# Weights by whole rows with the step in the lower word, sketches side by side, and the first batch's features beside its keys

## The chip, the cores and the metric

The kernel runs on one core of a Trainium2 chip. The metric is the device time of one execution in microseconds. Before the change the median is 358.86 us over three runs (357.6 to 360.12). An execution counts as slow here when it took over 1.5% longer than the fastest of the same kernel. In the profile before the change TensorE does the matrix products (busy 274.9 of 357.9 us), ScalarE and VectorE the element-wise work (153.8 and 250.4 us).

## The reference, cut to what matters

```python
# q, k, v: (batch 4, heads 4, seq 1088, head_dim 32) float32;  S1, S2: (8, 32) float64
def phi(x):                                   # degree-2 sketch: 64 features
    a = einsum('rd,bhsd->bhsr', S1, x)
    b = einsum('rd,bhsd->bhsr', S2, x)
    return einsum('bhsi,bhsj->bhsij', a, b).reshape(..., 64)
q_p, k_p = phi(q), phi(k)
num = q_p @ (k_p^T v);   den = q_p . sum(k_p) + 1e-6
x = num / den                                 # (4, 1088, 128)
theta = x @ w_theta                           # then the mixing over tokens:
y = w_tok_r @ (x * cos(theta)) + w_tok_i @ (x * sin(theta))     # two 1088 x 1088 matrices, float64
u = x + y
out = u + maximum(u @ w_ch, 0)
```

The denominator can be small, so the kernel computes it in exact slices of 16-bit numbers (names with `sl`, `cz`, `mv`, `lv`, `fl`, `dn`). Other names in the profiles: `cm` is the matrix made from the products of a batch's keys, `mv` the matrix for the denominators that is made from it, `kp` and `qp` the features of keys and queries, `zst` the phases, which are `x` times the cosine or the sine of theta. The two mixing matrices come as 8-byte floats, 17 rows of 128 x 1088. Each is turned into 4-byte floats on the chip, which is the first thing that the change touches.

## The kernel before

`load_f32` loads half a row of 544 columns. ScalarE reads the higher word of each float and writes its scaled value into `wT`, then writes two 16-bit halves of a correction, `step`, into a tile of its own, where the two halves of a column lie side by side. VectorE shifts `wT` by 3 bits and adds the step.

```python
def load_f32(dst, src):
    ...
    st = stg.tile([P, PIECE], I64, tag="st", name="st")[:p, :n]      # PIECE = 544, pool of 4
    nc.sync.dma_start(st, src)
    lo, hi = split(st)                                               # the two 4-byte words, 8 bytes apart
    step = stg.tile([P, PIECE, 2], I16, tag="step", name="step", bufs=2)[:p, :n]
    x = dst.bitcast(I32)
    A.activation(dst, hi.bitcast(F32), AF.Copy, scale=2.0**-112)
    A.activation(step[:, :, 1].bitcast(F16), hi.bitcast(F32), AF.Copy, scale=2.0**-60)
    A.activation(step[:, :, 0], lo.bitcast(U32), AF.Copy, scale=2.0**-29)
    ts(x, x, 3, ALU.logical_shift_left)
    tt(V, x, x, step.rearrange("p n t -> p (n t)").bitcast(I32), ALU.add)
...
    with level("first"):
        load(0, "kqv")
        ...                                     # S1, S2 in two tiles, each with its own small operations
        query_slices(0)
        matrices(0)                             # ends with mv
        keys_values(0, spare)
        attention(0)                            # features, denominators, then numerator and x by group
```

A tile framework schedules all this: the program gives levels of priority, and the framework fixes one order of instructions per engine. Each engine then works through its queue in that order: in the profile after the change, VectorE stands still for 2.90 us at one operation although the next one in its queue is ready.

## Time and profile before

| | before |
|---|---|
| time, median | 358.86 us |
| span of the profiled run | 357.9 us |
| ScalarE busy from 0 to 115.9 us | 86.80 us (75%) |
| VectorE busy in the same stretch | 92.05 us (79%) |
| first product of the mixing | 115.87 us |
| from there to the end | 242.0 us |

ScalarE's timeline in the steady stretch, one half row (columns: start, length, engine, line, output and input):

```profile
60.87 0.69 ACT L134 ACTIVATE wT<-st 128x544 f32<-128x544 f32 x1
61.47 0.80 ACT L135 ACTIVATE step<-st 128x544 f16<-128x544 f32 x1
62.13 0.79 ACT L136 ACTIVATE step<-st 128x544 int16<-128x544 uint32 x1
62.79 0.67 ACT L134 ACTIVATE wT<-st 128x544 f32<-128x544 f32 x1
```

A half row occupies ScalarE for 1.92 us here, from 60.87 to 62.79 (1.89 us for the next ones).

### The profile page before, as it was taken

How to read it: one execution, taken by the hardware profiler on the slowest of the kernel's cores; microseconds unless marked ns; L12 is line 12 of the kernel's file. 1: busy time of each engine (PE TensorE's matmuls, PEld its weight loads, DVE VectorE, ACT ScalarE, POOL GpSimd, SP SyncE). 2: the span in 40 equal slices, each digit the busy share in tenths (PEclk: the TensorE clock that was granted, in tenths of full speed). 3: DMA queues.
4: the chain of work that ended last, by engine and by line, in shares of the span. 5: the costliest groups of instructions: out<-in, count | busy, mean ns of one | idle time of the engine just before them, and what ended most of it. 6: DMA issues, size and time to landing. Idle time of an engine off the chain costs nothing.

```text
span 357.9 us, 4021 instructions
## 1 busy us (share of the span) xinstructions
PE 274.9 (77%) x1355; PEld 192.1 (54%) x1355; DVE 250.4 (70%) x713; ACT 153.8 (43%) x313; POOL 0.7 (0%) x6
## 2 busy tenths in 40 slices
PE   0406680145327999999689999996999999999994
PEld 0304480023226676776357777674777766776562
DVE  4898886985996699559948794896589569542111
ACT  0799729997958442061134413312335131332000
POOL 0000000000000000000000000000000000000000
PEclk9999955556555899999969999997899999999998
DMA  7668447883720012020010122000000000000010
GB/s 289 214 229 269 153 145 243 293 304 108 238 59 4 2 65 69 0 67 3 22 40 2 65 66 70 21 22 20 0 0 3 0 9 15 22 20 0 0 44 18
DMA packets 11604, 28.78 MB, mean 80 GB/s; under 512 B 1216, under 2 KB 5568, under 8 KB 11584
## 3 DMA queue, kind: packets, MB, share of 16 engines
q1 hardware_dynamic: 11376, 28.51, 24.3%
q8 instruction: 10, 0.16, 0.2%
q14 instruction: 10, 0.08, 0.1%
q10 hardware_dynamic: 208, 0.02, 0.0%
HBM read 26.30 MB, written 2.23 MB: 80 GB/s over the span
## 4 chain that ended last, share of the span: by engine, by line
PE 69%; DVE 17%; ACT 8%; DMA 3%; issue 1%; ACTq 0%
PE y L566 36%; PE w L519 4%; PE acc L398 3%; ACT step L135 3%; PE w L539 2%; PE y L576 2%; PE y L398 2%; PE w L446 2%; ACT step L136 2%; DVE wT L93 2%; PE w L513 2%; PE w L388 2%; DMA s_t_st<-s_t 2%; PE acc L306 2%; PE w L447 2%; PE w L534 1%
## 5 line engine op out<-in xcount | busy, mean ns | idle before, releaser
L566 PE MATMUL y<-wT,zst 128*128 128x384 f32 (+1 forms) x384 | 134.8, 481 | 1.4 <-DVE zst L93 1.4
L566 PEld LDWEIGHTS y<-wT,zst 128*128 128x128 f32 x384 | 68.1, 193 | 30.6 <-DVE zst L93 2.3
L585 ACT COPY ot<-y 128x384 f32<-128x384 f32 (+2 forms) x16 | 6.0, 398 | 62.1 <-PE y L580 62.1
L135 ACT ACTIVATE step<-st 128x544 f16<-128x544 f32 (+1 forms) x35 | 27.8, 795 | 4.3 <-DVE wT L93 4.2
L93 DVE CUSTOM_DVE_ANT_0 wT<-wT,step 128x1088 uint16<-128x1088 uint16 x34 | 24.4, 718 | 5.8 <-ACT step L136 5.8
L519 PEld LDWEIGHTS w<-kvbd,qpT 128*128 128x128 f32 x144 | 21.6, 213 | 11.3 <-ACT qpT L517 10.4
L136 ACT ACTIVATE step<-st 128x544 int16<-128x544 uint32 (+1 forms) x35 | 27.4, 784 | 0.0
L519 PE MATMUL w<-kvbd,qpT 128*128 128x64 f32 x144 | 23.4, 297 | 3.2 <-ACT qpT L517 3.1
L134 ACT ACTIVATE wT<-st 128x544 f32<-128x544 f32 x34 | 22.9, 685 | 2.3 <-DMA st<-w_tok 2.2
L517 ACT COPY qpT<-w 128x256 f32<-128x256 f32 x36 | 12.9, 367 | 24.6 <-PE w L513 24.5
L513 PE MATMUL w<-ident,qp 128*128 128x128 f32 x72 | 14.6, 304 | 7.7 <-DVE qp L93 7.6
L93 DVE TENSOR_TENSOR uT<-xT,y 128x384 f32<-128x384 f32 (+1 forms) x12 | 6.3, 529 | 19.2 <-PE y L566 19.1
L97 DVE TENSOR_SCALAR tn<-w 128x384 f32<-128x384 f32 x12 | 6.7, 557 | 17.8 <-PE w L539 17.8
L536 ACT COPY xT<-w 128x384 f32<-128x384 f32 x12 | 5.7, 475 | 29.8 <-PE w L534 29.8
L449 ACT COPY lv<-w 128x384 f32<-128x384 f32 x36 | 14.9, 504 | 8.3 <-PE w L448 8.2
L513 PEld LDWEIGHTS w<-ident,qp 128*128 128x128 f32 x72 | 10.1, 170 | 9.8 <-ACT wT L134 8.1
L97 DVE TENSOR_SCALAR wT<-wT 128x544 int32<-128x544 int32 x34 | 14.6, 435 | 0.0
L446 PE MATMUL w<-mv,q 128*128 128x384 f16 x36 | 13.4, 372 | 0.8 <-DVE mv L93 0.8
L398 PEld LDWEIGHTS acc<-ld_v,kp 128*128 128x128 f32 x108 | 13.0, 192 | 1.5
L539 PEld LDWEIGHTS w<-w,xT 128*128 128x128 f32 x72 | 10.6, 215 | 5.2 <-ACT xT L536 4.5
L404 ACT COPY kvbd<-acc 64x64 f32<-64x64 f32 x6 | 1.2, 206 | 27.6 <-PE acc L398 27.6
L100 DVE SCALAR_TENSOR_TENSOR fl<-lv 128x864 f32<-128x864 f32 x4 | 4.2, 1054 | 12.3 <-ACT lv L449 12.3
(230 smaller groups left out, 523.5 us busy)
## 6 DMA issues: line engine op xcount, KB each, us to landing
st<-w_tok SPq DMA_DIRECT2D x34, 544.0 KB, 4.6
ld_k<-k_l SPq DMA_DIRECT2D x4, 576.0 KB, 4.0
ld_q<-q_l SPq DMA_DIRECT2D x4, 576.0 KB, 4.4
ld_v<-v_l SPq DMA_DIRECT2D x4, 576.0 KB, 3.8
out<-ot SPq DMA_DIRECT2D x8, 192.0 KB, 2.1
out<-ot SPq DMA_DIRECT2D x4, 128.0 KB, 1.8
st<-w_sq SPq DMA_DIRECT2D x1, 256.0 KB, 4.6
out<-ot SPq DMA_DIRECT2D x4, 32.0 KB, 1.8
```

Of the source, the lines that this page charges most:

```text
L93: eng.tensor_tensor(out=o, in0=a, in1=b, op=op)
L97: V.tensor_scalar(out=o, in0=a, scalar1=s1, scalar2=s2, op0=op0, **kw)
L134: A.activation(dst, hi.bitcast(F32), AF.Copy, scale=2.0**-112)
L135: A.activation(step[:, :, 1].bitcast(F16), hi.bitcast(F32), AF.Copy, scale=2.0**-60)
L136: A.activation(step[:, :, 0], lo.bitcast(U32), AF.Copy, scale=2.0**-29)
L398: nc.tensor.matmul(kv[:, n], kp[:, i * H + 2 * n:i * H + 2 * n + 2].rearrange("p h i j -> p (h i j)"), vn[:, c, 2 * n:2 * n + 2].rearrange ...
L446: nc.tensor.matmul(lp, q0, flat[:, 0:4 * W], start=True, stop=False, skip_group_check=True)
L449: A.copy(lv[:, :, :, c].rearrange("p l t n -> p (l t) n"), lp.rearrange("p (x n) -> p x n", n=HR))
L513: nc.tensor.transpose(tr[:, n * P:(n + 1) * P], qp[:, i * H + 2 * n:i * H + 2 * n + 2].rearrange("p h i j -> p (h i j)"), ident)
L519: nc.tensor.matmul(num[:, i * P + n * 2 * D:i * P + (n + 1) * 2 * D], qpT[:, n], kvbd[b][:, n], start=True, stop=True)
L539: nc.tensor.matmul(th[:, i * P:(i + 1) * P], xT[:, i * P:(i + 1) * P], w2[:, 0], start=True, stop=True)
L566: nc.tensor.matmul(yp[:, :t1 - t0], z, wT[:, i, t0:t1], start=(i == 0), stop=(i == NK - 1))
```

## The change

It has three parts. The weights are converted by whole rows, and the step is written back into the lower word of the staged float, which saves the step tile. S1 and S2 lie side by side in one tile and share their small operations, and their loads come before those of q and v. For the first batch, everything that does not need its matrix (the level sums of two of the three outputs, half of the denominator's slices and all three groups of numerators) is placed ahead of that matrix. The diff holds some edits beside these: later batches make their matrix before they slice their queries, the slices of keys and queries share one buffer, and the phases use whole staged rows as buffers. The core of the diff, cut at the "..." lines:

```diff
-        st = stg.tile([P, PIECE], I64, tag="st", name="st")[:p, :n]        # pool of 4 half rows
+        st = stg.tile([P, S], I64, tag="st", name="st")[:p, :n]            # pool of 3 rows
-        step = stg.tile([P, PIECE, 2], I16, tag="step", name="step", bufs=2)[:p, :n]
+        step = st.bitcast(I16).rearrange("p (n t) -> p n t", t=4)
         A.activation(dst, hi.bitcast(F32), AF.Copy, scale=2.0**-112)
+        A.activation(step[:, :, 0], lo.bitcast(U32), AF.Copy, scale=2.0**-29)
         A.activation(step[:, :, 1].bitcast(F16), hi.bitcast(F32), AF.Copy, scale=2.0**-60)
-        A.activation(step[:, :, 0], lo.bitcast(U32), AF.Copy, scale=2.0**-29)
-        tt(V, x, x, step.rearrange("p n t -> p (n t)").bitcast(I32), ALU.add)
+        tt(V, x, x, lo, ALU.add)
 ...
-            for n in range(0, S, PIECE):
-                load_f32(wT[:, i, n:n + PIECE], w_tok[i][:, n:n + PIECE])
+            load_f32(wT[:, i], w_tok[i])
 ...
-        query_slices(0)
         matrices(0)
-        keys_values(0, spare)
-        attention(0)
+        query_slices(0)
+        features_s(0)                      # levels of the two outputs that need no matrix
+        denominator_slices(0, 1, 2)
+        keys_values(0, spare)
+        nums = [numerator(0, g, spare) for g in range(NG)]
+        features_n(0)
+        denominator_slices(0, 2, 3)
+        denominators(0)
+        for g in range(NG):
+            mixed(0, g, nums[g])
```

## The prediction

> **What bounds the kernel now.** I read the page first (busy shares, the 40 slices, the groups), then the stretches (windows), then the timeline of each engine over the first 130 us.
>
> ```profile
> PE   0406680145327999999689999996999999999994
> DVE  4898886985996699559948794896589569542111
> ACT  0799729997958442061134413312335131332000
> ```
>
> Each digit is the busy tenth of 9 us. There are two stages. Up to about 117 us TensorE is a third to half busy while ScalarE and VectorE turn the 8-byte weights into floats and prepare the first batch. After that TensorE is full (227 us busy of the 241 us from 117 us to the end). The stage before sets when the full stretch begins; its end is the first product with the batch's phases, here `zst`:
>
> ```profile
> 66.67 0.17 DVE L192 TENSOR_REDUCE mn<-acc 128x1 f32<-128x8 f32 x1
> 77.27 0.29 DVE L93 TENSOR_TENSOR mv<-nz,hmf 128x128 f16<-128x128 f16 x1
> 85.95 1.06 DVE L100 SCALAR_TENSOR_TENSOR fl<-lv 128x864 f32<-128x864 f32 x1 [3.08 <-ACT lv L449]
> 105.29 0.56 DVE L93 TENSOR_TENSOR x<-w,rd 128x384 f32<-128x384 f32 x1
> 115.25 0.56 DVE L93 TENSOR_TENSOR zst<-x,tn 128x384 f32<-128x384 f32 x1 [2.46 <-ACT tn L546]
> 115.87 2.92 PE L566 MATMUL y<-wT,zst 128*128 128x384 f32 x4 [1.23 <-DVE zst L93]
> ```
>
> Columns are start, length, engine, instruction, and the idle time before it. The batch's matrix `mv` is ready at 77.6, the features at 86.3 (ScalarE's last copy), the normalized `x` at 105.3, the mixing starts at 115.9. Between 85.9 and 105.3 VectorE has no idle time: its own queue is the path. Weights run through the same queues:
>
> ```profile
> L135 ACT ACTIVATE step<-st 128x544 f16<-128x544 f32 x34 | 27.3, 804 | 4.3 <-DVE wT L93 4.2
> L136 ACT ACTIVATE step<-st 128x544 int16<-128x544 uint32 x34 | 27.0, 793 | 0.0
> L93 DVE CUSTOM_DVE_ANT_0 wT<-wT,step 128x1088 uint16<-128x1088 uint16 x34 | 24.4, 718 | 5.8 <-ACT step L136 5.8
> L134 ACT ACTIVATE wT<-st 128x544 f32<-128x544 f32 x34 | 22.9, 685 | 2.3 <-DMA st<-w_tok 2.2
> L97 DVE TENSOR_SCALAR wT<-wT 128x544 int32<-128x544 int32 x34 | 14.6, 435 | 0.0
> ```
>
> That is 77 us of ScalarE and 39 us of VectorE in a stage of 117. The DMA waits (2.2 us) say that transfers do not bound it. TensorE is cold there:
>
> ```profile
> 48.56 5.79 PE L398 MATMUL y<-ld_v,kp 128*128 128x64 f32 x26
> 98.09 1.97 PE L519 MATMUL w<-kvbd,qpT 128*128 128x64 f32 x8
> 123.73 0.66 PE L519 MATMUL w<-kvbd,qpT 128*128 128x64 f32 x4
> ```
>
> Eight passes take 1.97 us at a granted clock of 0.50 (window 98 to 99). The windows print 1.00 before 44.9 us, but a pair of key products (384 and 256 columns) starts every 0.53 us at 34 us and every 0.27 us at 122 us, so TensorE is at half rate there too.
>
> [...] So the add of weight and step, which will read its step as pairs 8 bytes apart, should keep the pace that the trace shows (402 ns at 512 elements, 718 at 1088: 0.55 ns each). [...] The trace has it only on ScalarE reads: `wT<-st` at 256 and 544 columns took 409 and 685 ns, 0.96 ns a column, against 0.83 between dense ones (`tn<-tt`, 384 columns, 524 ns; `half`, 1152 columns, 1164 ns): nearly full rate. [...]
>
> **The change, part by part.**
>
> *Whole rows.* ScalarE, start to start in the steady stretch 60 to 78 us, takes 1.89 us for a half row (0.57, 0.66, 0.66), 3.79 for a row. At 1088 columns the same slopes give 1.08 + 1.29 + 1.29 = 3.65. But both halves of the step now lie in the word that is being read, so the third activation waits for the second to complete, where they overlapped by 0.13: back to 3.79. VectorE: shift 0.64 (0.36 for half), add 0.08 + 2176 x 0.55 = 1.29 (0.64 for half): 1.93 against 2.0, 1 us over 17 rows. So the per-row gain is about nothing. What changes is the buffers: a buffer is now free only after VectorE's add, not after ScalarE. Three buffers of a row, about 5 us to refill one (estimate: 1.1 MB at the 350 GB/s seen in full windows, and 2 us).
>
> *S1 and S2 side by side, and earlier.* Some 24 small VectorE instructions of 0.1 us go, and their loads come ahead of q and v: the activation that waits for them (8.1 us) may start near 6.3. The block of key products, which starts at 31.3, should start near 29.6.
>
> *First batch beside its keys.* No work is removed; 27 more small products and a second pass of eight short VectorE operations come (about 1 us). The denominator's first half and all three numerators move ahead of `mv`. I walked the changed order with the durations above:
> - `cm` on VectorE at 35.6 (was 37.4). From there to the first `kp` 18.7 us of VectorE work stand in the queue (it was 7.9), as three rows of weights and the first half of the slices now precede it: `kp` at 53.4, was 45.3.
> - The value products (36 passes of 0.22) end at 62.3, was 54.4.
> - Nine numerator chunks follow: two transposes 0.53 and four passes 0.98 each, 1.5 us, 13.6 us in all, cold: 76. ScalarE's nine copies stand together in its queue, so weights stop on it for some 11 us.
> - The products that lead to `mv` stand between the numerators in TensorE's queue; the scale for `mv` comes at 79 (was 70.2), `mv` at 88 (77.6): VectorE must also do three whole rows of weights in this stretch.
> - Features' last part: 27 products of 64 to 128 columns, 3.6 us, and three copies: 92.4 (was 86.3).
> - VectorE from there to `x`: 17.2 us by the same sum that gives 19.7 for the 19.3 measured before: 109.6. Then 10 us to `zst`, as before (105.3 to 115.3), with x of the second group ready at once. Mixing starts at about 120, 4 us later.
> - In the full stage TensorE is spared the third group's numerators (three chunks at the warm rate, about 0.9 each: 2.5 us), and VectorE has the second batch's key slices (3.2 us) done before `zst`, which helps the stretch at 172 to 183 us where TensorE idled and VectorE was the bound. About -3 us.
> Sum: 358.9 + 4 - 3 = about 360, less something for a walk that is probably too strict: each wait was taken in series.
>
> **The rivals.**
> (a) *The early numerators pay.* The 19 us of VectorE after the features lose their `qp` products (three of 0.87) and half of the slices; if the cold TensorE block hides behind weights that are due anyway, mixing starts near 106 to 108 and the time is 348 to 350. For it: VectorE idles 15 us before 105. Against it: the idle time only helps if the order lets weights in, and ScalarE's nine copies stand in one block.
> (b) *The strided step is slow.* [...] ScalarE's 2-byte writes, 8 bytes apart in place of 4, may do the same (they already cost 1.15 ns a column against 0.96 for the 4-byte ones). [...]
> (c) *Buffers starve ScalarE.* Four rows wait in turn for VectorE's add plus 5 us. I counted this; if VectorE gets to the adds later, 2 to 4 us more.
>
> **Range and chances.** The walk gives 360, rival (a) 349, rival (b) 369. Weights of about 50, 27 and 23 in 100, and a walk that leans to the late side, put the middle at 358.0 and the range at 348 to 369. Faster by over 2% (under 351.7) 0.25, slower by over 2% (over 366.0) 0.22, the rest 0.53.
>
> **What would show it.** Per step: the add's mean at 2176 elements (1.3 to 1.35 us[...]); the step activations at 1088 columns (about 1.4[...]); start of the first numerator product (63) and end of the last (76), at a granted clock of 0.50; last write of `mv` (88), first `x` (109), first mixing product (120); TensorE's idle time after mixing starts (13.6 us before). The prediction is wrong if mixing starts before 110 or after 128, or if TensorE's busy time after the start changes by more than 4 us, which would mean that the order of the later batches changed after all.

## More of the kernel before

The chain of work that ended last, as shares of the span by engine:

```profile
PE 69%; DVE 17%; ACT 8%; DMA 3%; issue 1%; ACTq 0%
```

## The result, and the profile after

The changed kernel takes 384.9 us (median of 4 runs, 384.52 to 385.4), against 358.53 us for the kernel before (4 runs). The ratio is 1.0731, with a 95% interval of 1.0689 to 1.0774. Ratios here are from fast runs alone, and not quite the ratio of the medians. The outputs are correct.

TensorE's and ScalarE's lines of the page's 40 slices (9.6 us each here), and its chain of work that ended last:

```profile
PE   3205246992400049999996999999699999999994
...
ACT  1999998939999884402312343151245241152000
...
PE 57%; ACT 29%; DVE 8%; DMA 2%; issue 2%; ACTq 0%
```

TensorE's full stretch begins in the sixteenth slice (it was the fourteenth, of slices of 8.9 us), and ScalarE is at 8 or 9 tenths from the second slice to the fifteenth, but for one in which the copies of the numerators stand. Its share of the chain went from 8% to 29%: the path to the mixing now runs through ScalarE. The groups that convert the weights, with different shapes kept apart (columns: busy us in total and mean ns of one, then idle time before them and what ended it):

```profile
L134 ACT ACTIVATE st<-st 128x1088 int16<-128x1088 uint32 x17 | 44.7, 2632 | 0.0
L135 ACT ACTIVATE st<-st 128x1088 f16<-128x1088 f32 x17 | 44.5, 2620 | 0.3
L92 DVE CUSTOM_DVE_ANT_0 wT<-st,wT 128x2176 uint16<-128x2176 uint16 x17 | 21.8, 1282 | 17.9 <-ACT st L135 17.9
L133 ACT ACTIVATE wT<-st 128x1088 f32<-128x1088 f32 x17 | 20.6, 1210 | 0.0
L96 DVE TENSOR_SCALAR wT<-wT 128x1088 int32<-128x1088 int32 x17 | 12.2, 717 | 6.5 <-ACT wT L133 6.5
```

By the slope before (1.15 ns a column, from 471 ns at 256 columns and 804 ns at 544), twice the columns should take each step activation from 0.80 to about 1.4 us. It takes 2.63 and 2.62. VectorE's add (1282 ns) and shift (717 ns) cost what the prediction said, but VectorE now waits 17.9 us for the step. ScalarE's timeline shows one row in place of the half row above:

```profile
43.75 2.63 ACT L135 ACTIVATE st<-st 128x1088 f16<-128x1088 f32 x1
46.12 1.23 ACT L133 ACTIVATE wT<-st 128x1088 f32<-128x1088 f32 x1
47.24 2.61 ACT L134 ACTIVATE st<-st 128x1088 int16<-128x1088 uint32 x1
49.89 2.61 ACT L135 ACTIVATE st<-st 128x1088 f16<-128x1088 f32 x1
```

From one `L135` to the next, 43.75 to 49.89, a row occupies ScalarE for 6.14 us; two half rows took 3.79 to 3.84. How this reaches the first batch is seen on VectorE's timeline near the end of the stage:

```profile
128.10 0.18 DVE L92 TENSOR_TENSOR rd<-rd,gm 128x36 f32<-128x36 f32 x1
131.19 1.29 DVE L92 CUSTOM_DVE_ANT_0 wT<-st,wT 128x2176 uint16<-128x2176 uint16 x1 [2.90 <-ACT st L135]
132.40 0.55 DVE L92 TENSOR_TENSOR x<-y,rd 128x384 f32<-128x384 f32 x1
...
143.98 0.56 DVE L92 TENSOR_TENSOR zst<-x,tn 128x384 f32<-128x384 f32 x1 [0.46 <-ACT tn L584]
```

`x` has its factor `rd` at 128.3, but an add of weights stands ahead of it in the queue, and that add waits 2.90 us for ScalarE. So a late row delays the attention behind it in the queue, though the attention does not need that row. Over all 17 adds, VectorE's waits for the step sum to the 17.9 us of the groups above. The mixing starts at 144.6, 28.7 us later than before. The rest of the time is shorter: 383.3 - 144.6 = 238.7 us, against 242.0.

### The profile page after: what moved, and what is told of

It is laid out like the page before. It is cut to its first block, busy times and chain, and to the rows that moved or that the text cites. A ratio compares the mean times of both kernels' runs of the same rounds, so it can differ in the third digit from the quotient of the medians.

```text
span 383.3 us, 3967 instructions
## 1 busy us (share of the span) xinstructions
PE 277.8 (72%) x1382; PEld 196.5 (51%) x1382; DVE 248.4 (65%) x673; ACT 190.1 (50%) x263; POOL 0.7 (0%) x6
## 4 chain that ended last, share of the span: by engine, by line
PE 57%; ACT 29%; DVE 8%; DMA 2%; issue 2%; ACTq 0%
PE y L604 30%; ACT st L135 11%; ACT st L134 11%; ACT wT L133 4%; PE acc L401 3%; PE w L552 3%; PE w L546 2%; PE w L577 2%; PE y L614 2%; PE w L391 2%; PE acc L309 2%; PE y L552 2%; DMA st<-w_sq 1%; PE w L457 1%; PE w L572 1%
## 5 line engine op out<-in xcount | busy, mean ns | idle before, releaser
L134 ACT ACTIVATE st<-st 128x1088 int16<-128x1088 uint32 (+1 forms) x18 | 45.5, 2527 | 0.0
L135 ACT ACTIVATE st<-st 128x1088 f16<-128x1088 f32 (+1 forms) x18 | 45.3, 2516 | 0.3
L92 DVE CUSTOM_DVE_ANT_0 wT<-st,wT 128x2176 uint16<-128x2176 uint16 x17 | 21.8, 1282 | 17.9 <-ACT st L135 17.9
L457 PE MATMUL w<-mv,qsl 128*128 128x384 f16 (+2 forms) x45 | 14.2, 334 | 9.6 <-ACT lv L468 6.2
L133 ACT ACTIVATE wT<-st 128x1088 f32<-128x1088 f32 x17 | 20.6, 1210 | 0.0
L96 DVE TENSOR_SCALAR wT<-wT 128x1088 int32<-128x1088 int32 x17 | 12.2, 717 | 6.5 <-ACT wT L133 6.5
L458 PE MATMUL w<-mv,qsl 128*128 128x288 f16 (+2 forms) x45 | 12.7, 300 | 4.7 <-DVE qsl L96 4.7
L577 PE MATMUL w<-w,xT 128*128 128x128 f32 x72 | 13.0, 325 | 3.8 <-ACT xT L574 3.8
L391 PEld LDWEIGHTS w<-s_bd,kT 128*128 128x128 f32 x72 | 11.0, 224 | 9.2 <-ACT kT L388 8.5
L552 PE MATMUL w<-kvbd,qpT 128*128 128x64 f32 x108 | 15.6, 271 | 0.0
L577 PEld LDWEIGHTS w<-w,xT 128*128 128x128 f32 x72 | 11.2, 227 | 8.4 <-ACT xT L574 8.0
```

What stands on the lines that cost most here:

```text
L92: eng.tensor_tensor(out=o, in0=a, in1=b, op=op)
L96: V.tensor_scalar(out=o, in0=a, scalar1=s1, scalar2=s2, op0=op0, **kw)
L391: nc.tensor.matmul(kf[:, i * H * 2 * R:(i + 1) * H * 2 * R], kT[:, i], s_bd.rearrange("p h r -> p (h r)"), start=True, stop=True)
L457: nc.tensor.matmul(lp, q0, m[:, 0:4], start=first, stop=False, skip_group_check=True)
L552: nc.tensor.matmul(num[:, i * P + n * 2 * D:i * P + (n + 1) * 2 * D], qpT[:, n], kvbd[b][:, n], start=True, stop=True)
L577: nc.tensor.matmul(th[:, i * P:(i + 1) * P], xT[:, i * P:(i + 1) * P], w2[:, 0], start=True, stop=True)
```

## The experiments

Ten kernels ran. Times are medians; "first zst of batch 2" is when VectorE starts the phases with which TensorE can begin the second batch's mixing. The kernel before ran beside each of them (medians 358.4 to 359.7), and each ratio is against its own neighbours. All profiled runs in this table are fast, except that of `after_halves_kx`. The columns from "first mixing" on are read from one profiled execution, which need not be the median one (it took 356.3 us in `own_pairs3_kx` and 353.6 us in `own_pairs3_late`). `own_pairs`, `own_apart`, `before_inplace` and `after_halves` ran on one chip, the later runs on another.

| kernel | time us | ratio to before (95%) | first mixing | first zst of batch 2 | span | span - mixing | span - zst 2 |
|---|---|---|---|---|---|---|---|
| before | 358.5 | 1 | 115.9 | 188.8 | 357.9 | 242.0 | 169.1 |
| changed kernel | 384.9 | 1.0731 (1.0689-1.0774) | 144.6 | 215.9 | 383.3 | 238.7 | 167.4 |
| own_pairs | 357.4 | 0.9990 (0.9912-1.0067) | 116.3 | 188.3 | 355.5 | 239.2 | 167.2 |
| own_apart | 388.1 | 1.0802 (1.0758-1.0846) | 140.6 | 217.9 | 386.9 | 246.3 | 169.0 |
| before_inplace | 383.6 | 1.0673 (1.0637-1.0709) | 139.1 | 211.5 | 381.4 | 242.3 | 169.9 |
| after_halves | 361.0 | 1.0041 (0.9985-1.0098) | 110.5 | 190.5 | 359.4 | 248.9 | 168.9 |
| own_pairs_kx | 357.9 | 1.0000 (0.9956-1.0044) | 116.4 | 187.0 | 355.1 | 238.7 | 168.1 |
| after_halves_kx | 361.5 | 0.9936 (0.9883-0.9988) | 109.8 | 187.4 | 360.7 | 250.9 | 173.3 |
| own_pairs3 | 355.5 | 0.9906 (0.9879-0.9933) | 119.1 | 185.0 | 353.8 | 234.7 | 168.8 |
| own_pairs3_late | 354.8 | 0.9897 (0.9866-0.9927) | 117.9 | 182.9 | 351.9 | 234.0 | 169.0 |
| own_pairs3_kx | 358.3 | 0.9987 (0.9948-1.0026) | 119.7 | 183.8 | 354.4 | 234.7 | 170.6 |

**Theory 1:** ScalarE's 16-bit writes are slow when they lie 8 bytes apart, and this alone costs the 26 us. **Rivals:** whole rows or the order of the first batch cost them; or it is writing in place, into the words that are being read. The first three runs, with `after_halves` and the probe, tell these apart.

### own_pairs: the step back in a tile of its own, packed

```diff
-        step = st.bitcast(I16).rearrange("p (n t) -> p n t", t=4)
+        step = stg.tile([P, S, 2], I16, tag="step", name="step", bufs=2)[:p, :n]
-        tt(V, x, x, lo, ALU.add)
+        tt(V, x, x, step.rearrange("p n t -> p (n t)").bitcast(I32), ALU.add)
# and the pool of staged rows from 3 to 2, to make room
```

> The changed kernel with one thing undone: the step goes back to a tile of its own, in which its two 16-bit halves are packed (written 4 bytes apart); rows stay whole, everything else stays. Theory 1 (16-bit writes 8 bytes apart are what ScalarE is slow at): the two step activations fall from 2.62 us to about 1.4 us each at 1088 columns (the 1.15 ns a column of the kernel before, plus its constant), a row takes ScalarE about 3.7 us in place of 6.1, mixing starts at 108 to 122 in place of 144.5, and the time is 346 to 362. Rival (whole rows, or the early numerators, are what costs): the step activations get faster or not, but mixing still starts after 135 and the time stays above 375.

Its groups, as above:

```profile
L134 ACT ACTIVATE step<-st 128x1088 int16<-128x1088 uint32 x17 | 24.0, 1414 | 0.0
L135 ACT ACTIVATE step<-st 128x1088 f16<-128x1088 f32 x17 | 23.9, 1404 | 0.0
L92 DVE CUSTOM_DVE_ANT_0 wT<-wT,step 128x2176 uint16<-128x2176 uint16 x17 | 21.8, 1283 | 4.2 <-ACT step L135 4.2
```

The step activations fall to 1.41 and 1.40 us, the mixing starts at 116.3, and the time is 357.4 us (three runs at 357.2 to 357.6, one at 362.0). With everything else of the change in place, the 26 us are gone, and the rival that blames rows or order has fallen. VectorE's add takes 1283 ns here and 1282 ns in the changed kernel: that it read its step 8 bytes apart there cost it nothing. Removing the slow form takes (2632 - 1414) + (2620 - 1404) = 2434 ns per row from ScalarE, 41.4 us over 17 rows. The windows up to the first mixing show 125.06 us of ScalarE in 144.6 us for the changed kernel and 85.55 in 116.3 here: 39.5 us less work and 11.2 us more idle time, whose difference is the 28.3 us of the start.

### own_apart: a tile of its own, halves still 8 bytes apart

```diff
-        step = st.bitcast(I16).rearrange("p (n t) -> p n t", t=4)
+        sp = stg.tile([P, S, 4], I16, tag="step", name="step", bufs=1)[:p, :n]
+        step = sp[:, :, 0:2]                       # the other half of each 8 bytes is unused
```

> The changed kernel with the step in a tile of its own, but its 16-bit halves still 8 bytes apart (half of the tile is unused). Tells the distance of the writes from writing into the word that is read. Theory 1 (distance): the step activations stay at 2.5 to 2.7 us at 1088 columns and the time stays at 380 to 390. Rival (writing in place, over the data being read, is what is slow): they fall to about 1.4 us and the time falls to 346 to 365.

```profile
L136 ACT ACTIVATE step<-st 128x1088 f16<-128x1088 f32 x17 | 45.3, 2663 | 0.0
L135 ACT ACTIVATE step<-st 128x1088 int16<-128x1088 uint32 x17 | 44.6, 2624 | 3.9 <-DVE wT L92 3.9
```

2.66 and 2.62 us, and 388.1 us in all. Writing in place is not the cause; the distance between the writes is.

### before_inplace: the kernel before with the step in the lower word only

```diff
# in the kernel before, half rows and all else kept
-        step = stg.tile([P, PIECE, 2], I16, tag="step", name="step", bufs=2)[:p, :n]
+        step = st.bitcast(I16).rearrange("p (n t) -> p n t", t=4)
# the integer half first, and the add reads lo
```

> The kernel before (half rows of 544, its own order) with only the step moved into the lower word of the staged weights. Theory 1: the step activations at 544 columns go from 0.80 us to about 1.35 us each (0.12 + 544 x 2.24 ns), ScalarE gets about 37 us more work (68 x 0.55), mixing starts 20 to 30 us later than 115.9 and the time is 376 to 392. Rival (only whole rows, or the order of the first batch, make it slow): the step activations stay below 0.9 us and the time stays at 356 to 362.

```profile
L135 ACT ACTIVATE st<-st 128x544 int16<-128x544 uint32 x34 | 48.4, 1424 | 0.0
```

1.42 us where it was 0.80 (the other one 1415 ns), a start of the mixing at 139.1 and 383.6 us: this one edit makes nearly the whole loss (1.0673 of 1.0731) without any other part of the change.

### probe: the write forms by themselves

The kernel before with single operations at the end of its program, four of each form. The scheduler spread them over the execution (ScalarE ran them from 31 to 213 us), so its total time, 401.29 us, means nothing; their own durations are what is read.

```diff
+    def act(o, i):
+        A.activation(o, i, AF.Copy, scale=0.5)
+    ...                                            # W = 960; d16, d32: views of one 8-byte tile
+        for _ in range(4): act(d16[2-byte step], near)         # h1
+        for _ in range(4): act(d16[4-byte step], near)         # h2
+        for _ in range(4): act(d16[8-byte step], near)         # h4
+        for _ in range(4): act(d16[16-byte step], near[:, :480])
+        ...                                        # 4-byte outputs, 8-byte reads, in place, VectorE
```

> The kernel before with a block of single activations and VectorE operations appended after the last batch, four of each form, 960 columns (480 where the step is 16 bytes), to measure the write forms by themselves; its time is of no use. If the distance of 16-bit writes alone decides (theory 1): ScalarE with a contiguous source takes about 0.9 to 1.2 us for 16-bit writes next to each other or 4 bytes apart (0.9 to 1.15 ns a column) and 2.1 to 2.3 us for 16-bit writes 8 bytes apart, whether it reads from another tile or from the words it writes into; 4-byte writes next to each other or 8 bytes apart take 0.9 to 1.1 us. Rival (the mix of an 8-byte read step and an 8-byte write step is what is slow, not the write): with a contiguous source the 16-bit writes 8 bytes apart stay under 1.3 us. For VectorE: if it has the same weakness, its 16-bit writes 8 bytes apart take twice what those 4 bytes apart do.

ScalarE's timeline has one of each contiguous-source form in the program's order, 16-bit outputs 2, 4 and 8 bytes apart:

```profile
107.82 1.00 ACT L715 ACTIVATE probe<-wT 128x960 f16<-128x960 f32 x1
127.31 1.32 ACT L715 ACTIVATE probe<-wT 128x960 f16<-128x960 f32 x1
132.72 2.42 ACT L715 ACTIVATE probe<-wT 128x960 f16<-128x960 f32 x1
```

The groups show 16-bit outputs 16 bytes apart (480 columns), 16-bit outputs into the words being read (960 columns, 8 bytes apart), 4-byte outputs next to each other or 8 bytes apart (960), and 4-byte outputs 16 bytes apart (480):

```profile
L715 ACT ACTIVATE probe<-wT 128x480 f16<-128x480 f32 x4 | 9.4, 2360 | 0.0
L715 ACT ACTIVATE probe<-probe 128x960 f16<-128x960 f32 x8 | 18.8, 2345 | 0.2
L715 ACT ACTIVATE probe<-wT 128x960 f32<-128x960 f32 x16 | 16.8, 1052 | 0.2
L715 ACT ACTIVATE probe<-wT 128x480 f32<-128x480 f32 x4 | 4.3, 1069 | 0.1
```

With 4-byte outputs a step of 8 bytes costs ScalarE little (1.09 us for 960 columns in the eight that also read from the probe's tile, against a mean of 1.05 us for the sixteen above, of which half lie next to each other and half 8 bytes apart), and with 16-bit outputs it costs much (2.36 to 2.42 us, against 1.00 next to each other), although the source is contiguous. Half as many columns at twice the step cost the same 2.36 us. So for 16-bit outputs the time grew with the bytes from first to last write: 1920, 3840 and 7680 bytes took 1.00, 1.32 and 2.36 to 2.42 us. 4-byte outputs pay too when they are spread further: 480 of them 16 bytes apart took 1.07 us, as long as 960 of them 8 bytes apart (1.09 us). VectorE's probes, 16-bit outputs 2, 4 and 8 bytes apart:

```profile
227.95 0.66 DVE L97 TENSOR_SCALAR probe<-wT 128x960 f16<-128x960 f32 x1
232.96 0.70 DVE L97 TENSOR_SCALAR probe<-wT 128x960 f16<-128x960 f32 x1
239.19 1.25 DVE L97 TENSOR_SCALAR probe<-wT 128x960 f16<-128x960 f32 x1
```

VectorE has the same weakness in writes of 16 bits, 8 bytes apart (1.25 us, against 0.70 at 4 bytes and 0.66 next to each other). The weights' path never asks that of it.

### after_halves: the change without its first part

```diff
# the changed kernel with the weights' path of the kernel before:
# half rows of 544, packed step in its own tile, pool of 4
# (the later batches' phases lie in half-row buffers again, too)
-            load_f32(wT[:, i], w_tok[i])
+            for n in range(0, S, PIECE):
+                load_f32(wT[:, i, n:n + PIECE], w_tok[i][:, n:n + PIECE])
```

> The changed kernel with the weights' path exactly as before: half rows of 544, the step in a tile of its own, four staging buffers. So the rest of the change alone: S1 and S2 side by side, and the first batch's levels, features and numerators beside its keys. Theory 1 with the walk of the prediction right: mixing starts near 118 to 122 (115.9 before) and the time is 354 to 362. Rival (a) of the prediction (the early numerators pay once the weights' path is not slowed): mixing starts at 106 to 110, the time is 346 to 351. Rival (the order of the first batch is what costs): above 370.

The mixing starts at 110.5, close to what rival (a) of the prediction named (106 to 108), and yet the time is 361.0 us, no better than before. Both the walk of the prediction and rival (a) assumed that an earlier start of the mixing is an earlier end. It was not: from the start to the end it took 248.9 us in place of 242.0. The windows (columns: busy us and number of instructions of each engine, granted clock of TensorE, DMA share, GB/s) show where it went. First `after_halves`:

```profile
160.00:170.00 10.00, 7.04 (x18) 2.75 (x16) 8.73 (x17) 1.70 (x4) 0.00 (x0) 0.74 0.14 40
170.00:180.00 10.00, 5.51 (x21) 4.12 (x22) 10.00 (x16) 1.65 (x5) 0.00 (x0) 0.50 0.06 17
180.00:190.00 10.00, 6.77 (x33) 4.90 (x33) 5.16 (x11) 2.97 (x6) 0.00 (x0) 0.56 0.00 0
```

TensorE had used up the first batch's products at 162, and the second batch's phases only came at 190.5. VectorE was the busy engine in between (10.00 of 10 us from 170 to 180), and TensorE's granted clock fell to 0.50. In these 30 us TensorE idled 10.7 us, and 4.8 us in the kernel before: the 5.9 us between them are most of the 6.9 us by which the stage grew. Starting the first batch's mixing 5.4 us earlier made this hole longer, as the second batch's phases came no earlier (190.5 against 188.8).

**Theory 2,** formed after this run: in the kernels of this study the second batch's phases, not the first product of the mixing, fix the end. The last two columns of the table are its evidence: in the fast runs the span less the first mixing varies from 234.0 to 248.9 us, the span less the second batch's first `zst` only from 167.2 to 170.6. This is a regularity and not yet a cause. The traces show it more tightly for the third batch: in the eight fast profiled runs without the kx edit below, its first `zst` comes 102.0 to 102.6 us before the end. So the table shows that the differences arise before these points; it does not show that the second batch's phases set the end.

### own_pairs3: three staged rows in place of two

```diff
# own_pairs, with a pool of 3 for staged rows; the first batch's phases share it
-            zz = stg.tile([P, S], I64, tag="st" if b else "z", name="zst", bufs=2 if b else 1).bitcast(F32)
+            zz = stg.tile([P, S], I64, tag="st", name="zst", bufs=3).bitcast(F32)
```

> As own_pairs, but with three staging rows in place of two (the first batch's phases share their tag). Tests rival (c) of the prediction, that buffers starve ScalarE: in own_pairs ScalarE sat idle 7.0 us for weights that were not there yet. If that costs on the path: the idle time falls to 2 to 3 us, mixing starts 2 to 4 us before 116.3 and the time falls by as much, to 353 to 356. Theory 2 (the second batch's phases set the end): the idle time falls, mixing starts earlier or not, and the time stays at 356 to 359, as the second batch's zst stays at 187 to 190.

ScalarE's wait for weights, 7.0 us in `own_pairs`, is gone. The mixing starts later (119.1 in place of 116.3), the second batch's `zst` comes earlier (185.0 in place of 188.3), and the time falls to 355.5 us, a ratio of 0.9906 to before. Neither expectation named this outcome as a whole: the time that theory 2 gave was wrong, since it assumed that the second batch would stay where it was. That the start moved one way and the end the other fits theory 2, but it says less than it seems to. In `own_pairs3` TensorE runs the second batch's key products (114.0 to 119.0) ahead of the first mixing, so that 4.3 us more of its work lies before this mark than in `own_pairs` (55.0 against 50.8 us) and 4.2 us less after it (220.8 against 225.0); in `own_pairs` they run from 122.3 to 124.7. The first batch's `zst` itself is only 1.6 us later (117.3 against 115.7). And `own_pairs` ran on the other chip, with a ratio whose interval overlaps this one, so what the third row alone is worth is not shown. Its windows, for comparison with `after_halves`:

```profile
170.00:180.00 10.00, 5.85 (x18) 2.93 (x19) 7.72 (x16) 2.12 (x5) 0.00 (x0) 0.63 0.20 56
180.00:190.00 10.00, 9.85 (x59) 7.72 (x58) 5.29 (x14) 3.42 (x9) 0.00 (x0) 0.86 0.01 2
```

The same hole, but by 180 us TensorE is busy again (9.85 of 10 us, where it was 6.77). This also says of rival (c), that buffers starve ScalarE: with two rows they cost it 7.0 us of idle time, and a third row took that away, but the first mixing started no earlier for it.

### The three kx runs: the third batch's key slices behind the second batch's denominators

```diff
-        kx = work.tile([P, NC, H, D], F32, tag="qx", name="kx", bufs=1)
+        kx = work.tile([P, NC, H, D], F32, tag="fl", name="kx", bufs=1)
```

With this tag the scaled keys need a buffer that the denominators free late, so their slices (about 5 us of VectorE) can't stand ahead of them.

> The changed kernel with packed step pairs (as own_pairs, 357.4 us) and one more edit: the scaled keys of a batch use the buffer of the level sums of the denominators, so the third batch's key slices can't be placed ahead of the second batch's denominators on VectorE. Theory 2 (in the kernels with a fast weights' path the second batch's phases set the end, not the first product of mixing: from the second batch's first zst to the end the runs so far took 167 to 170 us): the second batch's first zst comes at 183 to 186 in place of 188.3, first mixing stays within 2 us of 116, and the time is 352 to 355. Rival (the start of mixing sets the end, or the third batch then runs late): the time stays at 356.5 to 360.

> The same edit on the changed kernel with the weights' path of before (as after_halves, 361.0 us, where mixing starts at 110.5 and the second batch's first zst comes at 190.5). Theory 2: zst of the second batch at 184 to 188, the time 353 to 358, though mixing starts no earlier than in after_halves. Rival: time at 359.5 to 363 as in after_halves.

> own_pairs3 with the third batch's key slices kept behind the second batch's denominators on VectorE (the edit of own_pairs_kx, which moved the second batch's zst 1.3 us earlier and the time not at all). If VectorE's order before the second batch's zst still costs: zst at 180 to 184 and 351 to 354 us. Rival (the hole is set by the chain of waits between engines, not by those 5 us of slices): zst at 184 to 187 and 354.5 to 357 us.

None of these bears theory 2 out. In `own_pairs_kx` the `zst` came 1.3 us earlier, not 2 to 5, and the ratio is 1.0000. `own_pairs3_kx` brought it to 183.8, inside what was expected, but the time rose to 358.3 us. `after_halves_kx` brought it to 187.4 and its runs scattered from 354.9 to 364.4 us; four of six, the profiled one among them, are over 1.5% above the fastest and count as slow, so its ratio rests on two runs (354.9 and 357.9, inside what was expected, but too few to count). So a couple of microseconds of this `zst` are not a couple of microseconds of the end: the regularity holds to about 3 us. The kept traces show where the lead went in `own_pairs3_kx`: its third batch's first `zst` comes 5.1 us earlier than in `own_pairs3` (246.6 against 251.7), and its fourth batch's 1.2 us later (309.0 against 307.9). Why is left open.

### own_pairs3_late: the third part undone

```diff
# own_pairs3, first batch in the order of before
-        features_s(0)
-        denominator_slices(0, 1, 2)
         keys_values(0, spare)
-        nums = [numerator(0, g, spare) for g in range(NG)]
-        ...
+        attention(0)
```

> As own_pairs3 (packed step pairs, three staging rows, 355.5 us) with the third part of the change undone: the first batch's levels, features and numerators again come after its matrix, as in the kernel before. Tells what the third part is worth once the weights' path is not slowed. The prediction's view (the early order costs about 4 us before mixing and gives 3 us back later): within 1% of 355.5, first mixing some 3 us earlier than the 119.0 of own_pairs3. Rival (a) (the early numerators pay): 359 to 364, with the second batch's first zst 4 to 8 us later than the 185.0 of own_pairs3. Theory 2: whichever way the time goes, it goes with the second batch's first zst: the end follows it by 167 to 170 us.

354.8 us, a ratio of 0.9897, against 0.9906 with the early numerators: the intervals overlap nearly wholly. So the third part is worth nothing that these runs can see. The mixing started 1.2 us earlier without it, where 3 us had been expected, and the first batch's `zst` came at 117.3 us in both. Whatever pays is in the rest: packed pairs by whole rows with three rows staged, S1 and S2 side by side, and the edits to later batches; no run separates these. This kernel and `own_pairs3` beat the kernel before by 1.0% (both intervals lie below 1) and the changed one by about 8%.

## Why the prediction was wrong, point by point

The step that failed is "Whole rows". It said: "At 1088 columns the same slopes give 1.08 + 1.29 + 1.29 = 3.65", then 3.79 us with the wait, so "the per-row gain is about nothing". The slope of the step activations (1.15 ns a column) came from writes 4 bytes apart and was carried over to writes 8 bytes apart. Measured are 1.21 + 2.63 + 2.62 us, 6.14 us a row start to start. Over 17 rows that is 40 us more of ScalarE than predicted, of which 28 us reached the start of the mixing (144.6 against 116.3 in `own_pairs`, where the slow writes are gone).

The prediction looked hard at the step of 8 bytes, but at the wrong end of it. What it weighed was VectorE's *read* of the step. That the add would keep its pace there was the estimate ("The trace has it only on ScalarE reads"), and it came true (1.28 us for the add, 1.29 predicted). On ScalarE it drew its evidence from 8-byte *reads*, which cost little (0.96 ns a column, against 0.83 with dense sources). The layout's new feature on ScalarE was 8-byte *writes*, and half a sentence of rival (b) was given to them.

Rival (b) was therefore right in kind and wrong in place and size. Its own part, the add on VectorE, cost nothing (1282 ns, against 1283 ns packed in `own_pairs`). Its clause on ScalarE's 2-byte writes was the cause, measured at 2.4 us a row. What such writes cost was not shown in any trace at that time: the 369 us given to this rival were the estimate, and 16 us short.

The rest of the walk can be checked where the slow writes are removed. `own_pairs` is the change with fast weights:

| event, us | predicted | changed kernel | own_pairs |
|---|---|---|---|
| key products start | 29.6 | 31.7 | 28.4 |
| `cm` on VectorE | 35.6 | 36.9 | 32.3 |
| first `kp` | 53.4 | 64.8 | 48.5 |
| first batch's numerators | 63 to 76 | 74.5 to 87.8 | 60.0 to 72.5 |
| last write of `mv` | 88 | 100.5 | 86.0 |
| first `x` | 109.6 | 132.4 | 105.7 |
| first mixing product | 120 | 144.6 | 116.3 |
| from there to the end | 239 | 238.7 | 239.2 |
| time | 360 (sum), 358.0 | 384.9 | 357.4 |

- S1 and S2 side by side: the first activation waits until 5.7 us in place of 8.1 (6.3 expected), and in every profiled run with this edit it starts at 5.3 to 5.8. The key products start 2.9 us earlier than before in `own_pairs`, where 1.7 were expected, but at 31.7 in the changed kernel and 31.6 in `own_pairs3_late`, no earlier than before (31.3). So the loads were right, and a gain from them is not shown.
- First batch beside its keys: the events were right, and what they do to the start was not. The numerators take 12.5 us where 13.6 were expected, at the granted clock of 0.50 that was named, and the walk is 1 to 5 us late throughout, as it said it might be. But "Mixing starts at about 120, 4 us later" is no price of this order: against the kernel before, the start is 5.4 us earlier in `after_halves`, 0.4 later in `own_pairs` and 3.2 later in `own_pairs3`, and of the last, 2.0 us remain without the early order (`own_pairs3_late`).
- Full stage about 3 us shorter: right in size (238.7 and 239.2 against 242.0). In the two 240 us windows from the first mixing, TensorE's busy time fell from 228.67 to 224.92 us, inside the 4 us that the prediction allowed. Its reason, the numerators that are no longer done there, is not borne out: `own_pairs3_late` puts part of them back there, TensorE's work after the first mixing rises by 2.0 us (222.8 against 220.8), and the stage is no longer for it (234.0 against 234.7). So why the size came out right is not shown, and it may be luck; what the key slices give was not tried by itself.
- Rival (a), the early numerators pay: `after_halves` reached a start of 110.5, near its 106 to 108, and gained nothing, and `own_pairs3_late` is as fast without them. What fell with it is the premise of the whole prediction, that an earlier first mixing is an earlier end.
- Rival (c), buffers: ScalarE did not wait for staged rows in the changed kernel (no such wait is in its views), because it was the slow engine itself. In `own_pairs`, with two rows, it waited 7.0 us. The estimate of 5 us to refill a row held: on the page of the changed kernel a row of 1088 KB lands 5.0 us after its issue.
- Slips in its working, none of which decides anything: its own addends put the first `kp` at 54.3 (35.6 + 18.7), not at 53.4; ScalarE's last copy of the features ends at 85.9, not 86.3; VectorE idles 20.8 us before 105 us, and about 15 only when the first 10 us are left out; TensorE's idle time after the mixing starts is 13.3 us, not 13.6.

## What to carry to other kernels

When data is packed into a new layout, price the write side of each instruction as well as the read side, and take the price from an instruction with the same element size and the same distance between writes; a slope from half that distance was wrong by a factor of two here (1.29 us predicted for a step activation of 1088 columns, 2.63 and 2.62 us measured). Before a stage is moved earlier, look for the next hole after it: an early start that only let the busy engine run out of work sooner was worth nothing here (5.4 us earlier in `after_halves`, at a ratio of 1.0041). And look at queues that mix bulk conversion with a chain that others wait for: here a slower producer of the bulk held up the chain through VectorE's queue (2.90 us at one add), though the chain itself needed nothing from it.
